# Order of the first loads, an earlier pick and whole last rows in a fused sigmoid attention and mixture-of-depths kernel

## The chip, the cores and the metric

The kernel runs on one core of one Trainium2 chip. The time is the device time of that core in microseconds for one execution, with all loads from and stores to the chip's DRAM in it. The time before is the median of 4 runs, 437.7 us (436.35 to 439.9). A profile shows one more execution.

## The reference

Sigmoid attention is computed for 8 batches of 12 heads, 448 tokens and 64 dims in float32. Its result, put together to 768 columns per token, goes through a mixture of depths: of each batch the 128 tokens with the highest gate score get a two-layer perceptron added, and the other tokens pass through.

```python
# q, k, v: (8, 12, 448, 64); w_gate: (768,); w1: (768, 1024); w2: (1024, 768); capacity: 128
scores = scale * np.matmul(q, k.transpose(0, 1, 3, 2)) - np.log(S)
attn = 1.0 / (1.0 + np.exp(-scores))
x = np.matmul(attn, v)                    # to (B, S, H * D)
scores = np.einsum('bsd,d->bs', x, w_gate)
out = x.copy()
for b in range(B):
    top_idx = np.argpartition(-scores[b], capacity)[:capacity]
    xe = x[b, top_idx]
    h = np.maximum(xe @ w1, 0.0)
    ye = h @ w2
    g = 1.0 / (1.0 + np.exp(-scores[b, top_idx]))
    out[b, top_idx] = x[b, top_idx] + g[:, None] * ye
```

## The kernel before

Everything is written out in one order by hand (`stream`); each engine runs its own instructions in that order and waits on semaphores for what it needs.

Four heads make a quad; there are 24 quads, three to a batch. A stage `s` (0 to 11) works on two quads, 2s and 2s + 1, in seven slots `n`. In a slot `score` computes q times k for 128 rows of keys, half of them from the one quad and half from the other (`chunks` and `column` say which). A slot has four calls of it: `e` is the half of the 64 dims that is summed, `pr` the pair of heads in the quad; the two pairs lie on different rows of the matmul array. `squash` runs ScalarE's sigmoid on one pair's scores. `value` multiplies v with the sigmoids of earlier slots and gathers the result in four banks. So each slot from the fifth on holds score calls, value calls of slots some way back and two sigmoids. `turn` and `turn_first` transpose q and k on VectorE in blocks of 32; `take` transposes the results into `x_b`, from where `store` writes them to `out`.

In stage 0 the slots 0 and 1 use quad 0 alone and the slots 2 and 3 quad 1 alone, so the first slots can do with little data; `outs` is a pair of banks that slots 0 and 2 write, `PA` the pair that slots 1 and 3 write. After slot 3 the banks of `outs` become the banks of the results, and the first value calls are made. `turn_first` takes k in parts: parts 0 and 1 serve the first slots and the middle columns of k, part 2 the ends of k, needed from slot 4.

The perceptron is computed for two batches at a time, by a scheme of seven products in place of eight (`first`, `second`, `first_sums`, `second_sums`), in blocks after slot 3 of the later stages, and after the last stage in `rest`. Before it, `gate_part` and `gate` make a batch's gate scores, `rank` and `place` rank the tokens, `fetch` picks the 128 tokens by an index and `gather` fetches their rows by an indirect DMA on GpSimd's (POOL's) queue. `FETCHED` says after which slot each batch is picked. The results are added into these rows (`xe`), and `scatter` writes them back by another indirect DMA. For the last batch, `scatter_half` writes each half of the 768 columns as soon as its last sum is made.

All other loads go through SyncE's (SP's) queue in the order of the program. A DMA there waits in line for what its tile needs, and for one of eight semaphores: the ninth DMA waits for the first to land, the tenth for the second, and so on. At the start, SP's queue holds: the middle of k of quad 0, q of quad 0, the middle of k of quad 1, q of quad 1 (`load_first`), four blocks of v for the first columns, the ends of both k, four blocks with the rest of v, four gate-weight loads (`constants`), and then k and q of quads 2 and 3 and v of stage 1.

Of the kernel before, what the change touches and what calls it, by code (L numbers as in the profile page):

```python
# [17 lines left out]
def kernel(  # L18
# [89 lines left out]
    def load_first():  # L108

        raw, turned = {}, {}  # L110
        for i in range(2):
            if i:
                both = heads["both"] = moe.tile([P, 6 * KH * P], F32, name="rows_t")
                raw["k", i] = both[:, :TB * Dh]
            else:
                raw["k", i] = head.tile([P, TB * Dh], F32, name="raw_k", bufs=1)
            raw["q", i] = head.tile([P, TB * Dh], F32, name="qT")
            for which, src, at, n in (("k", k, AT, TB - 2 * AT), ("q", q, 0, TB)):
                heads[which, i] = raw[which, i]
                nc.sync.dma_start(  # L120
                    out=raw[which, i][:, at * Dh:(at + n) * Dh],
                    in_=bass.AP(tensor=src.tensor, offset=src.offset + (i * 4 * S + at) * Dh,
                                ap=[[TB * Dh, P], [1, n * Dh]]))
        load_v(0, True)
        for i in range(2):
            nc.sync.dma_start(
                out=raw["k", i].rearrange("p (r d) -> p r d", d=Dh)[:, 0:AT],
                in_=bass.AP(tensor=k.tensor, offset=k.offset + i * 4 * S * Dh,
                            ap=[[TB * Dh, P], [Dh, AT], [1, Dh]]))
            nc.sync.dma_start(  # L130
                out=raw["k", i].rearrange("p (r d) -> p r d", d=Dh)[:, TB - AT:],
                in_=bass.AP(tensor=k.tensor, offset=k.offset + (i * 4 * S + TB - AT) * Dh,
                            ap=[[TB * Dh, P], [Dh, AT], [1, Dh]]))
        load_v(0, False)

    def turn_first(i, *parts):

        t = heads["raw", i].rearrange("p (r e d) -> p e r d", e=2, d=TT)
        kt = heads["k", i]
        for part in parts:  # L140
            if part < 2:
                nc.vector.transpose(kt[:, :, 2 * part:2 * part + 2],
                                    t[:, :, AT + part:AT + part + NA + 2:NA + 1])
                nc.vector.transpose(kt[:, :, 2 * (NA + part):2 * (NA + part) + 2],
                                    t[:, :, NA + part:NA + part + 3:2])
                continue
            for a, r in ((0, 0), (1, TB - AT)):
                nc.vector.transpose(kt[:, :, 4 + a:2 * NA:2], t[:, :, r:r + AT])

    def open_first(i):  # L150
        heads["raw", i] = heads["k", i]
        heads["k", i] = head.tile([P, 2, TB, TT], F32, name="kT")

# [34 lines left out]
    def load_v(s, pairs_too=None):  # L188
# [12 lines left out]
        if s or pairs_too:  # L201
            raw_v[s] = t = t.rearrange("p (h c) -> p h c", h=4)

        def block(x, r, n):
# [126 lines left out]
    def constants():  # L331
        make_identity(nc, iden)
        for a in range(4):
            p = slice(a * TT, (a + 1) * TT)
            nc.sync.dma_start(
                out=wg_b[p],
                in_=bass.AP(tensor=moe_w_gate.tensor, offset=moe_w_gate.offset + a * TT,
                            ap=[[0, TT], [P, HP], [1, TT]]))
        nc.gpsimd.iota(slot_s, pattern=[[0, 1]], base=0, channel_multiplier=1,
                       allow_small_or_imprecise_dtypes=True)  # L340

        for t in (gate_s, *who):
# [11 lines left out]
        nc.gpsimd.tensor_scalar(out=tie, in0=tie, scalar1=slot_s, scalar2=-2.0 ** -126,  # L354
                                op0=ALU.is_lt, op1=ALU.mult)
        nc.gpsimd.tensor_scalar(out=wg_b, in0=wg_b, scalar1=GATE_UP, scalar2=None, op0=ALU.mult)

# [23 lines left out]
    def score(s, n, e, pr, out):  # L381

        for y in range(2):
            x, c, step = chunks(s, n, y)
            r = 2 * column(s, n, y)
            kt = heads["k", 2 * s + x]
            qt = heads["q", 2 * s + x].rearrange(
# [146 lines left out]
    def fetch(b):  # L534

        n = CAP
        idx = moe.tile([P, 1], I32, name="idx", bufs=7)
        got = moe.tile([P, 2], F32, name="got", bufs=5)
# [8 lines left out]
        gather(b)  # L547
        if b == B - 1:
            st[b]["halves"] = [moe.tile([P, 1], I32, name="idx", bufs=7) for _ in range(2)]
            for m in range(2):  # L550
                nc.vector.tensor_scalar(out=st[b]["halves"][m][:n], in0=got[:n, 0:1],
                                        scalar1=2.0, scalar2=float(2 * b * S + m),
                                        op0=ALU.mult, op1=ALU.add)

# [129 lines left out]
    def second_sums(p, key, ps):  # L684
        n = CAP
        left = pairs[p].setdefault("left", [6, 8])
        for x, m in QUARTERS[key]:
            b = 2 * p + x
            cols = slice(m * DH, (m + 1) * DH)
            xe = st[b]["xe"]  # L690
            nc.vector.scalar_tensor_tensor(  # L691
                out=xe[:n, cols], in0=ps[:n, :DH], scalar=st[b]["gate"][:n, 0:1],
                in1=xe[:n, cols], op0=ALU.mult, op1=ALU.add)
            left[x] -= 1
            if b == B - 1:
                parts = st[b].setdefault("parts", [4, 4])
                parts[m] -= 1
                if not parts[m]:
                    scatter_half(b, m)
            elif not left[x]:  # L700
                scatter(b)
# [7 lines left out]


    def scatter_half(b, m):
        n = CAP
        nc.gpsimd.indirect_dma_start(
            out=out[:b + 1].rearrange("b s (m d) -> (b s m) d", m=2),
            out_offset=bass.IndirectOffsetOnAxis(ap=st[b]["halves"][m][:n, 0:1], axis=0),
            in_=st[b]["xe"][:n, m * DH:(m + 1) * DH], in_offset=None)

# [150 lines left out]
    def slot(s, n):  # L868


        if s == 0 and n < NF + 1:
# [3 lines left out]
            psc = PA if n % 2 else outs  # L875
            for e in range(2):
                for pr in (1, 0):
                    score(s, n, e, pr, psc[pr])
            for pr in (1, 0):
                squash(s, n, pr, psc[pr])  # L880
# [105 lines left out]
    def after(s, n):  # L986
# [35 lines left out]
        if s == 0:  # L1022
            if n == 0:
                open_first(1)
                turn_first(1, 0)
# [6 lines left out]
            if n == 4:  # L1032
                turn("k", 2, 3)
                load_v(1)
                load("k", 4)
            if n == 5:
                turn("q", 2, 3)
        if (s, n) in WEIGHTS:
            m, x = WEIGHTS[s, n]
# [19 lines left out]
    RANKED = [(3, 1), None, (6, 1), None, (9, 0), None, (11, 6)]  # L1059
    FETCHED = {(3, 6): 0, (5, 2): 1, (6, 3): 2, (8, 3): 3, (9, 5): 4, (11, 3): 5}  # L1060

    first_outs = ExitStack()

    def stream():
# [4 lines left out]
        nc.vector.memset(bias_s, NEG_LOG_S)  # L1069
        open_first(0)  # L1070
        turn_first(0, 0)
        turn("q", 0)
        turn_first(0, 1)
        pool = first_outs.enter_context(tc.tile_pool(name="ps_o", bufs=1, space=PSUM))
# [47 lines left out]
```

## Time and profile before

| What | Value |
|---|---|
| median of 4 runs | 437.7 us |
| those runs | 436.35, 436.59, 438.82, 439.9 us |
| the profiled execution's own time | 438.38 us |
| its span | 436.6 us |
| granted TensorE clock, mean | 0.994 |
| busy: PE, DVE, ACT, POOL | 424.1, 281.6, 190.9, 49.0 us |
| moved by DMA | 78.64 MB, 180 GB/s in the mean |

PE is TensorE, DVE VectorE, ACT ScalarE, POOL GpSimd and SP SyncE. The span reaches from the first to the last instruction, and the profiled execution's own time is 1.8 us longer. A line of the timeline gives the start, the duration from start to end of the merged instructions, engine, line of the kernel, operation, tiles, shapes and count, and in brackets the engine's idle time before it with what ended it. The chain is the work that ended last, followed back from the end, each piece with its start and length. A line of the table by stretches gives the stretch, its length, the busy time and instruction count of PE, its weight loads, DVE, ACT and POOL, then the granted clock, the busy share of the DMA engines and the GB/s.

### The profile page before, as it was taken

Reading aid. Unit: us, or ns where it says so; the run is one execution under the profiler, and the core shown is the slowest. Engines: PE = TensorE matmul, PEld = TensorE weight load, DVE = VectorE, ACT = ScalarE, POOL = GpSimd, SP = SyncE. Lnnn points to the kernel's source line nnn. Section 1 sums busy time; section 2 is a strip of 40 time slices with the busy share of each in tenths; the row PEclk is TensorE's granted clock in tenths of the full one; section 3 lists DMA queues with packets and bytes.
Section 4 is the critical chain, followed back from the end, with each engine's and each line's share of the span. In section 5 each row is a group of like instructions: output and inputs, shape, how many; then the busy total and the mean of one; then the engine's idle time right before and its main releaser. Section 6 shows DMA issues by size and latency. Waiting matters only on the chain.

```text
span 436.6 us, 14255 instructions
## 1 busy us (share of the span) xinstructions
PE 424.1 (97%) x6324; PEld 253.7 (58%) x6324; DVE 281.6 (64%) x598; ACT 190.9 (44%) x249; POOL 49.0 (11%) x82
## 2 busy tenths in 40 slices
PE   6999999999999999999999999999999999999994
PEld 2565454534666468565447549546445749669852
DVE  3335556792958785976968736755765749982561
ACT  4566666656664642650561661563264330101100
POOL 3000001210110020100202020010020110101002
PEclk9899999999999999999999999999999999999998
DMA  7696837899863998989466896399834990921001
GB/s 211 200 240 203 296 87 142 219 185 248 230 197 80 202 286 254 215 290 225 163 209 196 248 222 140 110 269 268 259 101 98 243 258 24 182 60 74 0 1 72
DMA packets 114985, 78.64 MB, mean 180 GB/s; under 512 B 91436, under 2 KB 100908, under 8 KB 114924
## 3 DMA queue, kind: packets, MB, share of 16 engines
q1 hardware_dynamic: 107948, 62.47, 54.7%
q0 software_dynamic: 3344, 9.54, 7.6%
q10 hardware_dynamic: 3632, 5.74, 5.5%
q8 instruction: 49, 0.80, 0.8%
q14 instruction: 12, 0.10, 0.1%
HBM read 57.25 MB, written 20.48 MB: 178 GB/s over the span
## 4 chain that ended last, share of the span: by engine, by line
PE 93%; DMA 3%; ACT 1%; issue 1%; DVE 0%; SPq 0%; POOLq 0%; ACTq 0%
PE a L391 30%; PE o L423 28%; PE o L616 11%; PE o L680 11%; PE a L616 6%; PE a L680 5%; DMA qT<-in_q_dram 2%; ACT attn L405 1%; PE o L580 1%; PE p L391 1%; DMA out_dram<-xe,idx 1%; DMA out_dram<-attn,idx 1%; PE a L580 0%; SPq L120 0%; POOLq L1117 0%
## 5 line engine op out<-in xcount | busy, mean ns | idle before, releaser
L391 PE MATMUL a<-qT,kT 32*64 32x448 f32 x2624 | 243.1, 539 | 0.4
L405 ACT ACTIVATE attn<-a,bias_s 128x896 f32<-128x896 f32 x162 | 161.7, 1008 | 84.7 <-PE a L391 82.0
L423 PE MATMUL o<-attn,raw_v 32*64 32x448 f32 x1952 | 176.5, 537 | 0.1
L391 PEld LDWEIGHTS a<-qT,kT 32*64 32x64 f32 x2624 | 95.1, 132 | 89.4 <-ACT attn L405 52.9
L423 PEld LDWEIGHTS o<-attn,raw_v 32*64 32x64 f32 x1952 | 69.8, 131 | 28.9 <-issue 23.6
L447 DVE STREAM_TRANSPOSE x_b<-o 128x448 f32<-128x448 f32 x48 | 28.1, 626 | 52.7 <-PE o L423 34.9
L423 PE MATMUL o<-attn,rows_t 32*64 32x448 f32 x448 | 42.2, 538 | 0.8 <-issue 0.8
L632 ACT ACTIVATE hidden<-hidden 128x512 f32<-128x512 f32 x12 | 7.5, 632 | 65.8 <-DVE hidden L629 55.6
L458 DVE TENSOR_REDUCE gate_p<-scr 128x14 f32<-128x448 f32 x48 | 29.8, 621 | 1.7
L629 DVE TENSOR_TENSOR hidden<-o,hidden 128x512 f32<-128x512 f32 x23 | 15.2, 688 | 23.9 <-PE o L616 23.7
L455 DVE TENSOR_TENSOR scr<-x_b,wg_b 128x448 f32<-128x448 f32 x48 | 29.6, 617 | 1.1
L379 DVE STREAM_TRANSPOSE kT<-raw_k 128x448 f32<-128x448 f32 x42 | 24.1, 612 | 7.3 <-PE a L391 7.0
L370 DVE STREAM_TRANSPOSE qT<-qT 128x896 f32<-128x896 f32 x22 | 23.9, 1086 | 6.2 <-DMA qT<-in_q_dram 6.2
L616 PE MATMUL o<-rows_t,spare 128*128 128x128 f32 x216 | 25.6, 276 | 0.0
L616 PEld LDWEIGHTS o<-rows_t,spare 128*128 128x128 f32 x216 | 24.8, 192 | 1.4 <-DVE x_b L447 1.4
L680 PE MATMUL o<-spare,hidden 128*128 128x384 f32 x72 | 24.3, 487 | 0.0
L513 DVE SCALAR_TENSOR_TENSOR scr<-rep,who,tie 128x448 f32<-128x448 f32 (+1 forms) x28 | 19.0, 677 | 7.4 <-DMA rep<-scores 6.6
L691 DVE SCALAR_TENSOR_TENSOR xe<-o,gate,xe 128x384 f32<-128x384 f32 x29 | 16.6, 612 | 9.7 <-PE o L680 9.6
L529 POOL DMA_DIRECT2D ranks<-turned x28 | 14.6, 527 | 70.6 <-DVE turned L526 70.6
L423 PEld LDWEIGHTS o<-attn,rows_t 32*64 32x64 f32 x448 | 16.4, 131 | 7.6 <-issue 7.4
L423 PE MATMUL o<-attn,hidden 32*64 32x448 f32 x224 | 20.2, 535 | 0.0
L616 PE MATMUL o<-rows_t,w_sb 128*128 128x128 f32 x168 | 20.0, 276 | 0.1
(118 smaller groups left out, 392.7 us busy)
## 6 DMA issues: line engine op xcount, KB each, us to landing
qT<-in_q_dram SPq DMA_DIRECT2D x24, 448.0 KB, 5.0
out_dram<-x_b SPq DMA_DIRECT2D x32, 336.0 KB, 8.5
raw_k<-in_k_dram SPq DMA_DIRECT2D x21, 448.0 KB, 5.1
spare<-sum SPq DMA_DIRECT2D x18, 384.0 KB, 6.3
sum<-spare SPq DMA_DIRECT2D x8, 768.0 KB, 7.9
raw_v<-in_v_dram ACTq DMA_DIRECT2D x24, 224.0 KB, 6.6
w_sb<-in_moe_w_dram SPq DMA_DIRECT2D x6, 768.0 KB
rows_t<-in_v_dram SPq DMA_DIRECT2D x8, 224.0 KB, 4.4
```

The costliest lines, as they stand in the source:

```text
L370: nc.vector.transpose(heads["q", i], heads["q", i])
L379: nc.vector.transpose(kt[:, e], t[:, e].rearrange("p (a n) d -> p n a d", a=2))
L391: nc.tensor.matmul(out[y * Dh:(y + 1) * Dh, h % 2, :S], kt[d, e, r:r + 2].rearrange("d r t -> d (r t)"), qt[d, e], start=(e == 0), stop=(e ...
L405: nc.scalar.activation(a, psc[:, :, :S], AF.Sigmoid, bias=bias_s, scale=QK_SCALE)
L423: nc.tensor.matmul(PO[x][pr][j * Dh:(j + 1) * Dh, :S], raw_v[s][rows, 2 * pr + j, at:at + Dh], attn[s, pr, n][rows, j, :], start=((s, x, p ...
L447: nc.vector.transpose(x_tiles[b][:, :, 2 * g + pr, :], PO[x][pr][:, :S].rearrange("p (r t) -> p r t", t=TT))
L455: nc.vector.tensor_tensor(out=tmp, in0=x_tiles[b][:, :, hp, :], in1=wg_b[:, hp:hp + 1, :].to_broadcast([P, TB, TT]), op=ALU.mult)
L458: nc.vector.tensor_reduce(out=gate_parts[b][:, :, hp], in_=tmp, axis=AX.X, op=ALU.add)
L513: nc.vector.scalar_tensor_tensor(out=junk[:n], in0=rep[:n], scalar=own, in1=tie[:n], op0=ALU.subtract, op1=ALU.is_gt, accum_out=place_s[:n ...
L616: nc.tensor.matmul(ps[:, f, :n], w((t * FH + f) * P, P), x[:, t, :n], start=(t == 0), stop=(t == KH - 1))
L680: nc.tensor.matmul(ps[:n, :DH], h[:, t, :n], w(t * DH, DH), start=(t == 0), stop=(t == FH - 1))
L691: nc.vector.scalar_tensor_tensor(out=xe[:n, cols], in0=ps[:n, :DH], scalar=st[b]["gate"][:n, 0:1], in1=xe[:n, cols], op0=ALU.mult, op1=ALU ...
```

## The change

The loads at the start are put in another order. k of quad 1 is loaded whole in one DMA. v is issued after q of quad 0 has been transposed: `load_v` writes one element of v's tile on VectorE, behind these transposes, and the DMA waits for that. The two ends of quad 0's k and the rest of v follow. The gate weights are loaded after slot 4 of stage 0 (`gate_weights`), behind k and q of quads 2 and 3, and v of stage 1 after slot 0 of stage 1, behind q and k of quads 4 and 5.

In slots 0 to 3 of stage 0 the score calls run pair by pair (both halves of the dims of one pair, its sigmoid, then the other pair), where they ran half by half.

Batch 5 is picked after slot 2 of stage 11, where it was slot 3. The last batch's rows are written back by one scatter of whole rows after the last sum, and the two index tiles for the halves go.

```diff
 def load_first():
...
-            for which, src, at, n in (("k", k, AT, TB - 2 * AT), ("q", q, 0, TB)):
+            for which, src, at, n in (("k", k, 0 if i else AT, TB if i else TB - 2 * AT),
+                                      ("q", q, 0, TB)):
...
+    def load_second():
+
         load_v(0, True)
-        for i in range(2):
+        t = heads["k", 0].rearrange("p (r d) -> p r d", d=Dh)
+        for r in (0, TB - AT):
             nc.sync.dma_start(
-                out=raw["k", i].rearrange("p (r d) -> p r d", d=Dh)[:, 0:AT],
-                in_=bass.AP(tensor=k.tensor, offset=k.offset + i * 4 * S * Dh,
-                            ap=[[TB * Dh, P], [Dh, AT], [1, Dh]]))
-            nc.sync.dma_start(
-                out=raw["k", i].rearrange("p (r d) -> p r d", d=Dh)[:, TB - AT:],
-                in_=bass.AP(tensor=k.tensor, offset=k.offset + (i * 4 * S + TB - AT) * Dh,
+                out=t[:, r:r + AT],
+                in_=bass.AP(tensor=k.tensor, offset=k.offset + r * Dh,
                             ap=[[TB * Dh, P], [Dh, AT], [1, Dh]]))
         load_v(0, False)
...
 def load_v(s, pairs_too=None):
...
+        if pairs_too:
+            nc.vector.memset(t[:1, 0, :1], 0.0)
...
 def constants():
         make_identity(nc, iden)
-        for a in range(4):
-            ... (the four loads of wg_b)
...
+    def gate_weights():
+
+        for a in range(4):
+            ... (the four loads of wg_b)
         nc.gpsimd.tensor_scalar(out=wg_b, in0=wg_b, scalar1=GATE_UP, scalar2=None, op0=ALU.mult)
...
 def fetch(b):
-        idx = moe.tile([P, 1], I32, name="idx", bufs=7)
+        idx = moe.tile([P, 1], I32, name="idx", bufs=5)
...
         gather(b)
-        if b == B - 1:
-            st[b]["halves"] = [moe.tile([P, 1], I32, name="idx", bufs=7) for _ in range(2)]
-            for m in range(2):
-                nc.vector.tensor_scalar(out=st[b]["halves"][m][:n], in0=got[:n, 0:1],
-                                        scalar1=2.0, scalar2=float(2 * b * S + m),
-                                        op0=ALU.mult, op1=ALU.add)
...
 def second_sums(p, key, ps):
             left[x] -= 1
-            if b == B - 1:
-                parts = st[b].setdefault("parts", [4, 4])
-                parts[m] -= 1
-                if not parts[m]:
-                    scatter_half(b, m)
-            elif not left[x]:
+            if not left[x]:
                 scatter(b)
...
 def slot(s, n):      # s == 0 and n <= NF
-            for e in range(2):
-                for pr in (1, 0):
+            for pr in (1, 0):
+                for e in range(2):
                     score(s, n, e, pr, psc[pr])
-            for pr in (1, 0):
                 squash(s, n, pr, psc[pr])
...
 def after(s, n):     # s == 0
             if n == 4:
                 turn("k", 2, 3)
-                load_v(1)
+                gate_weights()
                 load("k", 4)
...
+        if (s, n) == (1, 0):
+            load_v(1)
...
-    FETCHED = {(3, 6): 0, (5, 2): 1, (6, 3): 2, (8, 3): 3, (9, 5): 4, (11, 3): 5}
+    FETCHED = {(3, 6): 0, (5, 2): 1, (6, 3): 2, (8, 3): 3, (9, 5): 4, (11, 2): 5}
...
 def stream():
-        open_first(0)
         turn_first(0, 0)
         turn("q", 0)
+        load_second()
         turn_first(0, 1)
```

## The prediction

> **What bounds the kernel now.** I read the page's head and chain first, then the chain piece by piece at both ends, then the timeline of the first 17 us, then the table by stretches for the clock.
>
> ```profile
> span 436.6 us, 14255 instructions
> PE 424.1 (97%) x6324; PEld 253.7 (58%) x6324; DVE 281.6 (64%) x598; ACT 190.9 (44%) x249; POOL 49.0 (11%) x82
> PE 93%; DMA 3%; ACT 1%; issue 1%; DVE 0%; SPq 0%; POOLq 0%; ACTq 0%
> ```
>
> TensorE (PE) is busy 97% of the span and 93% of the chain. Work taken off the other engines in the middle is worth nothing; what can be won lies where the chain leaves PE. There are two such places, the first 16 us and the last 11 us. The start:
>
> ```profile
> 2.12 7.95 DMA qT<-in_q_dram
> 10.09 0.66 DVE qT L375
> 10.88 3.08 PE p L391 x30
> 13.98 1.92 ACT attn L405 x2
> 15.94 1.01 PE o L423 x16
> ```
>
> The second q (I call it q1) is issued at 2.12 and lands at about 10.06. Its first half is transposed, the scores of slot n=2 run, two sigmoids follow, and only then do the first value matmuls start (15.94). From there PE has no large holes.
>
> ```profile
> 10.88 3.12 PE L391 MATMUL p<-qT,kT 32*64 32x448 f32 x32 [2.13 <-DVE qT L375]
> 13.98 1.91 ACT L405 ACTIVATE attn<-p,bias_s 128x896 f32<-128x896 f32 x2 [3.00 <-PE p L391]
> 7.70:11.10 3.40, 1.27 (x32) 0.44 (x24) 1.52 (x4) 3.28 (x4) 0.00 (x0) 1.00 0.86 185
> 11.10:14.50 3.40, 3.40 (x45) 1.67 (x39) 1.86 (x7) 0.52 (x1) 0.00 (x0) 0.51 0.54 137
> ```
>
> PE stood 2.13 us for q1, and ScalarE (ACT) then stood 3.00 us for PE. The two lower lines are stretches: PE was busy 1.27 of 3.40 us, and in the stretch after it the granted clock was 0.51, so slot 2 took 3.1 us where slot 0 took 1.76. The late q1 is paid twice. The end:
>
> ```profile
> 424.98 0.63 DVE xe L691
> 425.61 0.27 issue
> 425.88 3.02 DMA out_dram<-xe,idx
> ...
> 428.93 0.73 issue
> 429.66 2.52 DMA out_dram<-attn,idx
> ...
> 432.23 0.51 issue
> 432.74 1.20 POOLq L1117
> 430.14 0.62 DVE L691 SCALAR_TENSOR_TENSOR attn<-o,gate,attn 128x384 f32<-128x384 f32 x1 [1.44 <-PE o L680]
> 432.96 0.97 POOL L713 DMA_INDIRECT out_dram<-attn,idx  x1 [2.33 <-DMA out_dram<-attn,idx]
> ```
>
> Three scatters stand in a row, each waiting for the landing of the one before. The last rows are ready at 430.76 (430.14 + 0.62), but their second half goes out at 432.96, because the first half had to land.
>
> **The start, step by step.** SP's queue sends k0's middle, q0, k1's middle, q1 and then four blocks of v, 160 KB each, at 2.59 to 4.69. After the change k1 goes whole (448 KB for 256) and v waits for a memset of one element behind q0's transposes. These end at 5.95 (4.78 + 1.17), so v is issued from about 6.1 and, by today's 2.10 us for four issues, until 8.2. Behind the waiting v on SP stand k0's two ends, the rest of v, k2, k3, q2, q3.
>
> *q1.* k0, q0, k1 and q1 are 1,638 kB (decimal) then. By the one-us stretches the queues moved 23, 311, 357, 278 and 302 kB up to 6.0, which is 1,271; the rest at 300 per us is through at 7.2. What lies between bytes moved and landing: q0 (with k0, 721 kB, through at 4.1) landed by 4.78, 0.7 later, with little but plain loads in flight; q1 today (1,442 kB, through at 6.6) landed 3.5 later, with v in flight. So 7.9 by the one, 10.7 by the other. The new q1 resembles q0's case; I take 7.9 to 8.5.
>
> *ACT then sets the pace.* Its first sigmoid starts at 7.28, and four follow each other at 0.90, to 10.99. Slots 2 and 3 can follow without a hole if slot 2's first pair is ready at 10.99. It needs two transposes (0.7 to PE's start) and two score calls: 0.75 + 0.75 + 0.2 for draining, so landing + 2.5; that holds up to 8.5. Slot 2's sigmoids end at 10.99 + 2 x 0.90 = 12.8 instead of 15.9, and the first values start 3.1 earlier. PE's hole falls from 2.13 us to about 0.5, so I expect no halved clock.
>
> The clock has a rule against it: the Trainium skill, "TensorE: Matmul & The Clock Gate", section "HAM oscillation", says that gaps must exceed about 3.4 us to throttle. This trace halved it after 2.13 us. By the rule the drop had another cause and may stay: slot 3 would cost up to 1.4 more, and the sum would be about 1.4 higher. The measured row decides for me.
>
> *Order of the score calls.* The first four slots now do both halves of one pair, then of the other. The pairs use different row groups of PE: slot 0's 32 matmuls start in four groups of eight (5.48, 5.91, 6.28, 6.66), and both pairs are ready at the end, 7.24. If each pair keeps its own rows, pair 1 is ready at 7.2 as now, pair 0 about 0.5 later, behind the other pair's sigmoid of 0.9: nothing. If pair 1 gets the whole array, 0.4 is won. If PE does not look past pair 1, a slot takes 3.0 instead of 1.5 and the front gain is gone. Score and value matmuls of different rows, which alternate in the timeline at 18.02 and 18.10, say that it looks ahead; I take 0.
>
> *v and k0's ends.* v (655 kB) follows q1 at today's mean of 6 to 10 us (289, 187, 216, 238: 232 per us): 7.2 + 2.8 = 10.0, and with 0.7 to the landing 10.7; needed at 12.8. k0's ends (197 kB) 0.9 later: 11.6, and 0.89 + 0.64 for four transposes: 13.1; slot 4 needs them at 13.7. No price. The upper bound goes by today's latencies: 8.2 from issue to landing for v puts it at 15.8; the ends issued at 5.38 served the transpose at about 13.2, 7.8 later, which puts them at 16.6 and the transposes at 18.1, 4.4 too late. The first estimate is nearer, because those 8.2 are spent behind k1 and q1. A rule against it: "DMA: Bandwidth & Descriptors", "Rules for kernel authors", advises issuing a DMA early and waiting late. By it v should stay ahead, and by the upper bound the sum would lose 3.0.
>
> *Gate weights and next v.* Four gate-weight issues (12.76 to 15.47) leave the path of k2; their first reader on VectorE (DVE) was at 42.49: nothing. The next v is moved behind q4, q5 and k5. q4 waits for slot 6's scores (today 26.7, then 23.6), k5 for k4's transpose (24.9), so v is issued at 25.3 to 28. It ends a run of 2,294 kB from 24.6; at 290 per us that is 32.5, with latencies of 8.2 at most 36. Its first reader is at 38.82 today, 35.7 then. Cover 3 us, price 0 to 0.3.
>
> **Middle.** The pick of batch 5 (0.64, 0.69 and 0.15 on DVE) moves from 334.12 into DVE's idle 7.70 us before 331.56. Its gather went out at 336.36, and the six transposes that need it started at 343.53, as the 48 matmuls before them ended: nothing won here, safety gained, and POOL has nothing else to do then. Dropping two tiny DVE index instructions: nothing.
>
> **The end.** One scatter replaces two. It waits for the batch-6 scatter (landed 428.9, earlier than needed) and for the last row update, 430.76; with the 0.29 seen between DVE and POOL it goes out at 431.05, 1.9 before today's 432.96. From there to the span's end were 3.64; a whole row set took 3.02 to land where a half took 2.52, so 4.14: 435.2, a gain of 1.4. Bounds: by the median of such scatters in traffic (3.5) 0.9; with equal landings 1.9.
>
> **Sum.** The profiled execution took 438.38 (span 436.6 and 1.8 around it). 438.38 - 3.1 - 1.4 = 433.9. It is 0.7 above the median of the runs shown, 437.7; carried over to that, 433.2, 1.0% less. About 1% is also what a measurement of this kernel can tell from no change.
>
> **Rivals.** (a) *The start gives back half.* q1 keeps part of its lag and lands at 9.6, so ACT starts slot 2 at 12.1: 1.9 instead of 3.1, or the ends of k0 are a microsecond late. For it: the last parts of a load lag when others are in flight (k1 took until 8.27). Against: v is out of its way. 437.7 - 1.9 - 1.4 = 434.4. (b) *The end gives nothing*: the whole rows take 1.9 longer than a half. Against: 3.02 beside 2.52. 437.7 - 3.1 = 434.6. (c) *v and k0's ends become the wait*, at slots 3 and 4, by the upper bounds: slot 4 starts at 18.1 instead of 16.92, 1.2 later than today; PE stands some 3 us again, and a halved clock over 3.4 us costs 1.7; less 1.4 at the end: 439.2. It decides from v landing after 12.8 and takes the whole gain when the ends' transposes pass 16.9; if the next v is late by the same share it goes on to 442 or more. For it: 640 KB are issued 3.5 us later. Against: the queues are busy either way. (d) *v is not held*: the built order has the wait on DVE at the first v, so this is excluded.
>
> **Numbers.** Forecast 0.55, (a) 0.22, (b) 0.10, (c) 0.13. The forecast lies at the 1% line and its own range is 431.5 to 434; I count 0.48 of it as over 1%, since a shorter last landing or an earlier first sigmoid only add, and 0.07 within. (a) gives 0.05 and 0.17, (b) 0.01 and 0.09, (c) 0.11 slower and 0.02 within. Faster 0.54, same 0.35, slower 0.11. The range, 431.3 to 438.2, holds the forecast, (a), (b) and the milder part of (c).
>
> **What would show it.** Right: the first value matmul at 12.8 to 13.3; no q1 in the chain with more than 6.5 us; clock 1.0 between 11.1 and 14.5; ACT without a hole from 7.28 to about 14.6; one scatter of the last rows issued 0.3 after DVE's last update. Wrong: a PE wait on raw_v or on k0's transposes between 12 and 18 us, a hole before 35.7 at the next v, slots 0 to 3 of 3 us each, or a last landing over 4 us.

## The result, and the profile after

The changed kernel takes 435.42 us (median of 42 runs; 437.93 for the kernel before on the same chip, 68 runs). The ratio is 0.995, with a 95% interval of [0.9934, 0.9966]: 0.5% less, some 2.2 us, where 4.5 were forecast. In two later sets of runs the same kernel gave 0.9895 [0.986, 0.9931] and 0.9935 [0.9906, 0.9963], so the gain is somewhere between 2 and 5 us. The second set's 4.6 us is of the forecast's size; the pieces below show that the forecast's working fails all the same.

Its profiled execution took 433.96 us. The head and the chain of its page:

```profile
span 432.1 us, 14249 instructions
PE 424.3 (98%) x6324; PEld 253.7 (59%) x6324; DVE 281.4 (65%) x597; ACT 190.5 (44%) x249; POOL 48.1 (11%) x81
PE 94%; ACT 2%; DMA 1%; issue 1%; DVE 0%; POOLq 0%; SPq 0%; ACTq 0%
```

PE does the same work; the span is 4.5 shorter. That this is just the number forecast is chance: the pieces below make 2.1 by stage 1, less 0.6, and 1.6 at the end, and the other 1.4 was won between 45 and 320 us, where the two kernels are the same. The start, from the chain of waits:

```profile
1.18 3.47 DMA qT<-in_q_dram
5.38 2.87 PE p L397 x28
8.27 3.70 ACT hidden L411 x4
11.97 1.90 ACT attn L411 x2
13.92 1.01 PE o L429 x16
```

The second q has left the chain, and ScalarE's sigmoids run without a hole from 8.27 to the first values at 13.92 (15.94 before): 2.0 won, not 3.1. PE's clock was first granted in full at 7.6 us (4.3 before), so slot 0's scores took 2.87 where 1.76 was reckoned with. The end, from the timeline:

```profile
427.26 0.62 DVE L691 SCALAR_TENSOR_TENSOR attn<-o,gate,attn 128x384 f32<-128x384 f32 x1 [1.44 <-PE o L680]
428.16 0.96 POOL L700 DMA_INDIRECT out_dram<-attn,idx  x1 [4.19 <-DVE attn L691]
```

One scatter, issued 0.28 after the last row update (427.88); from PE's last product to the span's end it is 5.41 us, before it was 6.98. In between, at slot 4 of stage 1, the new kernel lost 0.6 that the forecast did not have:

```profile
37.11 1.65 PE L429 MATMUL o<-attn,rows_t 32*64 32x448 f32 x12
39.34 1.01 ACT L411 ACTIVATE attn<-a,bias_s 128x896 f32<-128x896 f32 x1 [1.35 <-PE a L397]
40.83 1.01 ACT L405 ACTIVATE attn<-a,bias_s 128x896 f32<-128x896 f32 x1 [0.73 <-PE a L391]
```

The timeline has twelve value matmuls with no scores among them, and ScalarE is idle for 1.35 us before the next sigmoid. The last line is the same sigmoid in the kernel before, with 0.73 idle before it. From stage 1's first sigmoid to this one it is 12.80 us, before 12.19.

### The profile page after: what moved, and what is told of

It reads as the page before. It is cut to its first block, busy times and chain, and to the rows that moved or that the text cites. A ratio compares the mean times of both kernels' runs of the same rounds, so it can differ in the third digit from the quotient of the medians.

```text
span 432.1 us, 14249 instructions
## 1 busy us (share of the span) xinstructions
PE 424.3 (98%) x6324; PEld 253.7 (59%) x6324; DVE 281.4 (65%) x597; ACT 190.5 (44%) x249; POOL 48.1 (11%) x81
## 4 chain that ended last, share of the span: by engine, by line
PE 94%; ACT 2%; DMA 1%; issue 1%; DVE 0%; POOLq 0%; SPq 0%; ACTq 0%
PE a L397 30%; PE o L429 29%; PE o L616 11%; PE o L680 11%; PE a L616 6%; PE a L680 5%; ACT attn L411 1%; PE o L580 1%; ACT hidden L411 1%; DMA qT<-in_q_dram 1%; DMA out_dram<-xe,idx 1%; PE p L397 1%; PE a L580 0%; POOLq L1105 0%; DVE x_b L453 0%
## 5 line engine op out<-in xcount | busy, mean ns | idle before, releaser
L616 PEld LDWEIGHTS o<-rows_t,w_sb 128*128 128x128 f32 x168 | 19.4, 192 | 1.0 <-DVE x_b L453 0.7
```

The lines of the kernel that those rows point to most:

```text
L616: nc.tensor.matmul(ps[:, f, :n], w((t * FH + f) * P, P), x[:, t, :n], start=(t == 0), stop=(t == KH - 1))
```

## The experiments

There are seventeen runs, two to four of them on one chip with the kernel before beside them; four are repeats. A ratio is good to about 0.3%, 1.3 us, so single terms below that were read in the profiles, one for each run. The table holds what I read there, in us. "Slot 4" is the start of that slot's first sigmoid in stage 0; "6 to 1.0" goes from slot 6's first sigmoid to stage 1's first, "1.0 to 1.4" from there to the first sigmoid of stage 1's slot 4 (the "five slots" of the expectations; 12.19 where nothing is lost), "tail" from the start of PE's last product to the end of the span.

| kernel | q1 transposed | first sigmoid | slot 4 | 6 to 1.0 | 1.0 to 1.4 | tail |
|---|---|---|---|---|---|---|
| before | 10.09 | 7.28 | 19.08 | 3.37 | 12.19 | 6.98 |
| after | 9.38 | 8.27 | 17.06 | 3.37 | 12.80 | 5.41 |
| e1_tail | 8.10 | 6.99 | 15.78 | 4.60 | 12.19 | 5.42 |
| e2_front | 10.03 | 7.61 | 17.71 | 3.37 | 13.53 | 6.99 |
| e3_halves_first | 8.76 | 7.10 | 16.44 | 3.37 | 14.07 | 5.41 |
| e4_no_hold | 10.98 | 7.73 | 20.08 | 3.37 | 13.21 | 5.42 |
| e5_after_again | 10.88 | 7.02 | 19.94 | 3.37 | 13.76 | 5.40 |
| e6_v1_early | 9.73 | 7.56 | 17.41 | 3.37 | 12.19 | 5.41 |
| e7_v1_early_halves | 9.04 | 7.96 | 16.72 | 3.37 | 12.19 | 5.41 |
| e8_tail_again | 9.30 | 7.09 | 16.98 | 5.62 | 12.90 | 5.41 |
| e9_best_again | 8.70 | 7.55 | 16.38 | 3.37 | 12.19 | 5.41 |
| e10_gates_early | 10.36 | 7.92 | 18.04 | 3.37 | 12.19 | 5.41 |
| e11_k1_split | 6.93 | 7.34 | 16.03 | 3.36 | 12.19 | 5.42 |
| e12_old_first_loads | 8.86 | 7.91 | 16.61 | 3.37 | 12.18 | 5.41 |
| e13_v1_one_later | 7.12 | 7.06 | 15.75 | 3.37 | 13.08 | 5.41 |
| e14_tail_gates_late | 9.51 | 7.32 | 17.19 | 3.37 | 12.19 | 5.42 |
| e15_after_third | 8.38 | 7.26 | 16.05 | 3.37 | 13.18 | 5.40 |
| e16_v1_behind_k4 | 11.32 | 7.52 | 20.42 | 3.37 | 12.19 | 5.41 |
| e17_v1_behind_k4_spent | 7.68 | 7.63 | 16.33 | 3.37 | 13.70 | 5.41 |

### The change in two halves: e1_tail, e2_front

e1_tail is the kernel before with one scatter of the last rows:

```
-            if b == B - 1:
-                ... (parts, scatter_half)
-            elif not left[x]:
+            if not left[x]:
                 scatter(b)
```

> The kernel before with one change: the last rows go back by one scatter. First theory (the end gains what the sum said, and it is the start that gains less over many executions than in the two profiled ones): 1.4 to 1.6 us less than before, ratio 0.9965, the scatter issued 0.9 after batch 7's last update and the span ending some 4.1 after that. Second theory (the end is what was overrated, and the start gains its 2 to 3 in nearly every execution): 0 to 0.5 less, ratio 0.999 to 1.000.

e2_front is the changed kernel with the halves and the old pick again, so that only the loads and the order of the scores are new:

```
+            if b == B - 1:
+                ... (parts, scatter_half)
-    FETCHED = {..., (11, 2): 5}
+    FETCHED = {..., (11, 3): 5}
```

> The changed kernel with the two half scatters and the later pick put back, so that the order of loads and of score calls alone is left. First theory: about 1.0 us less than before (ratio 0.9975), because the kernel before does not always lose what its profiled execution lost at its start. Second theory: 2 to 2.5 less (ratio 0.995).

Measured: e1_tail 0.9982 [0.9958, 1.0006], e2_front 1.0005 [0.9975, 1.0035]. The tail is 5.42 against 6.99, so the scatter is worth 1.57, and the column shows the same in every profile. The loads won nothing that the times show. e1_tail's profile says why; its start is the old code, and its sigmoids read:

```profile
6.99 1.90 ACT L405 ACTIVATE hidden<-p,bias_s 128x896 f32<-128x896 f32 x2 [4.21 <-PE p L391]
8.79 1.91 ACT L405 ACTIVATE hidden<-a,bias_s 128x896 f32<-128x896 f32 x2
10.68 1.90 ACT L405 ACTIVATE attn<-p,bias_s 128x896 f32<-128x896 f32 x2
12.47 1.91 ACT L405 ACTIVATE attn<-a,bias_s 128x896 f32<-128x896 f32 x2
15.78 1.01 ACT L405 ACTIVATE attn<-a,bias_s 128x896 f32<-128x896 f32 x1 [1.40 <-PE a L391]
```

No hole in the first eight sigmoids, no halved clock, slot 4 at 15.78: the start that I forecast for the change, made by the start code of the kernel before. The profiled execution of the kernel before, at 19.08, had been a bad draw.

### Parts of the start undone: e3_halves_first, e4_no_hold

Both are the changed kernel; e3_halves_first has the score calls half by half again, e4_no_hold lacks the memset that holds v back.

```
-            for pr in (1, 0):
-                for e in range(2):
+            for e in range(2):
+                for pr in (1, 0):
                     score(s, n, e, pr, psc[pr])
```

> The changed kernel with the score calls of slots 0 to 3 half by half again, as before. If the order of the calls is neutral, as the sum had it: the same as the changed kernel, ratio 0.995 to before. If pair by pair costs time where PE is at half clock (slot 0 took 3.09 in the profiled execution and ACT started at 8.27, not at 7.28): 0.5 to 1 faster than the changed kernel, ratio 0.993.

```
-        if pairs_too:
-            nc.vector.memset(t[:1, 0, :1], 0.0)
```

> The changed kernel without the memset, so that v is issued at 2.6 us, behind q1 and not behind q0's transposes; k1 still whole, the rest as changed. If v in flight is what makes q1 late: q1 lands at about 10.5 again, the first values start at 15 to 16 and the ratio is 0.998, near what the end alone gives. If q1's lag has another origin (packets that take about 1 us each already before v flows): q1 within 0.5 of 9.4, first values as in the changed kernel, ratio 0.995.

Measured: 0.9946 [0.9917, 0.9975] and 0.9964 [0.9934, 0.9995], beside 0.995 for the changed kernel. The order of the calls is worth nothing that shows. e4_no_hold had a late q1 (10.98) and a halved clock; one profile could not say whether that was the missing hold or a draw. All four profiles so far with the late next v had 12.8 to 14.1 in the column "1.0 to 1.4".

### The next v at its old place: e5_after_again, e6_v1_early, e7_v1_early_halves, e8_tail_again

e5_after_again and e8_tail_again repeat the changed kernel and e1_tail. The other two:

```
             if n == 4:
                 turn("k", 2, 3)
+                load_v(1)
                 gate_weights()
                 load("k", 4)
...
-        if (s, n) == (1, 0):
-            load_v(1)
```

e7_v1_early_halves also has the score calls half by half, as in e3_halves_first.

> The changed kernel again, nothing edited, on the same chip as the three runs beside it. Theory: the start of one execution is a draw. The forecast's 3.1 us at the start came from a profiled execution of the kernel before that had drawn badly (second q transposed at 10.09, slot 4's first sigmoid at 19.08, halved clock); other executions with the same start code reach slot 4 at 15.8. Then the changed kernel stays at its 2 us gain, ratio 0.993 to 0.997, of which 1.6 is the tail (5.4 us from PE's last product to the span's end), and in this new profile slot 4's first sigmoid falls somewhere between 16 and 18.5, not at 17.06 again. Rival: the start gain is real and the middle takes it back: slot 4 again at 17.0 to 17.2, a ratio like before, and the loss at the next v again at 12.8 us for five slots.

> The changed kernel with the next v issued at its old place (stage 0, slot 4, ahead of the next k), all else changed. Theory: the late next v costs 0.6 to 1.9 us, because its four blocks land at 33 to 36 us and five slots of stage 1 take 12.8 to 14.1 us in the profiles so far where the kernel before took 12.2. Then those five slots take 12.0 to 12.4 here, PE doesn't wait for it, and the time is 0.6 to 1.9 us below that of the changed kernel run beside it, about 434. Rival: the slow slots belong to something else that arrives late there (q4, q5 or k5, which now queue behind v again): five slots still take over 12.7, and the time is that of the changed kernel within 0.5.

> As the run with the next v at its old place, and the score calls of the first slots half by half again instead of pair by pair. Theory: the order of the calls is worth 0 to 0.5 us and the next v 0.6 to 1.9, and they add: 433.5 to 434.5, the fastest of these. Rival: the order of the calls matters not at all, as the forecast had it, and this agrees with its neighbour within 0.4.

> The kernel before with one whole scatter of the last rows in place of two halves, again, as a second look at its start, which is the old one. Theory: the start is a draw, the old code included; slot 4's first sigmoid lies anywhere from 15.8 to 19.1, its first full clock anywhere from 4 to 8 us, and the time is 1.0 to 1.6 below the kernel before by the tail alone (5.4 us from PE's last product to the end, for 7.0). Rival: the first look (slot 4 at 15.78) was the lucky one and the late q the rule: slot 4 at 18.5 or later with a halved clock behind it, and what the changed kernel has on this run, 1 to 2 us, is its start.

Measured: 0.9895 [0.986, 0.9931], 0.9917 [0.9883, 0.9951], 0.9893 [0.9859, 0.9928] and 0.994 [0.991, 0.9971]. The times don't separate them, though the profiles do: 12.19 in both with v early, 13.76 in the changed kernel beside them. The expected 434 for e6_v1_early was met (434.2), the order by time was not, since e5_after_again came out faster (432.6). As for the start, the same code that had slot 4 at 17.06 had it at 19.94 in e5_after_again, with q1 at 10.88 and a halved clock, while the old code was at 16.98 in e8_tail_again. There a second price appeared, in the column "6 to 1.0". DVE's timeline of e8_tail_again, and then of the changed kernel:

```profile
21.73 1.11 DVE L370 STREAM_TRANSPOSE qT<-qT 128x896 f32<-128x896 f32 x1
25.62 1.11 DVE L370 STREAM_TRANSPOSE qT<-qT 128x896 f32<-128x896 f32 x1 [2.78 <-DMA qT<-in_q_dram]
```

```profile
20.28 2.06 DVE L376 STREAM_TRANSPOSE qT<-qT 128x896 f32<-128x896 f32 x2
```

In the one, q3 lands 2.8 us after DVE is free, and the scores of stage 1's first slot (the expectations call it slot 7) wait for it: 5.62 instead of 3.37. In the other, both are there. In e8_tail_again q2 and q3 were issued at 15.94, behind four gate-weight issues that held SP from 13.05 to 14.93; in the changed kernel at 13.56. (Whether the issues' time or their packets delayed q3 the more is not told apart.) In the profiles with the old place, this wait is hidden where the start is late (19.08 at slot 4) and paid where it is early (15.78 and 16.98).

### Which part of the start matters: e9 to e12

The base is e7_v1_early_halves, run again as e9_best_again. e10_gates_early puts the four gate-weight loads back into constants(), ahead of k2. e11_k1_split splits the second k again:

```
-            for which, src, at, n in (("k", k, 0 if i else AT, TB if i else TB - 2 * AT),
+            for which, src, at, n in (("k", k, AT, TB - 2 * AT),
...
 def load_second():
+        for i in range(2):
+            ... (both ends of k0, then of k1)
```

e12_old_first_loads does that too, without the memset, and calls load_second() right behind load_first(), so that SP issues the first loads in the order of the kernel before.

> The version with the next v at its old place and the score calls half by half, unchanged, as the base for the three runs beside it. The five slots of stage 1 up to slot 4 take 12.19 us again, q3's transpose follows q2's at once, and the tail is 5.41; ratio to the kernel before 0.986 to 0.993. If it comes out above 0.995 the first look was a good draw.

> The base with the four gate-weight loads back ahead of the loads for stage 1 on SP's queue, as in the kernel before. Theory: what the start gains is not the first q but these four issues, 1.9 to 3.0 us on SP, which leave the path of k2, k3, q2 and q3. In the two profiles that had the old place and an early start, q3's transpose came at 23.4 and 25.6 and slot 7's scores waited for it (from slot 6's first sigmoid to stage 1's first, 4.60 and 5.62 us instead of 3.37). So here the same wait appears, q3 is transposed 2 us or more after q2 instead of right behind it, 4.0 to 5.5 instead of 3.37, and the run is 0.7 to 2 us slower than the base. Rival, the forecast's own step: the gate weights cost nothing there, 3.37 again and the base's time within 0.5.

> The base with the second k split again: its middle ahead of the second q, its two ends behind the held v. 98 KB each of 128 x 192 then leave the path of the second q. Theory: the hold's gain for the second q is eaten by loading the second k whole; with the split it is transposed at 8.0 to 9.0 instead of 8.8 to 10.9 (mean of six profiles 9.6), the ends still land before slot 4 needs them, and the run is 0.3 to 0.8 us faster than the base. Rival: the second q's lag comes from single slow packets on some DMA queues, whatever the bytes ahead: 8.8 to 10.9 again, and the base's time within 0.5.

> The base with the first loads as in the kernel before: second k split, v issued right behind the second q with nothing held, all else as in the base. Theory: over nine profiles the second q is transposed at 8.1, 9.3 and 10.1 with these loads and at 8.8 to 10.9 with the held ones, so the hold wins nothing: 8 to 10.5 here and the base's time within 0.7. Rival, the forecast: v in flight delays the second q by 2 us, its transpose is at 10 or later, slot 2's first sigmoid at 13 or later, and the run is 2 to 3 us slower than the base.

Measured: 0.993 [0.9907, 0.9954], 0.9917 [0.989, 0.9944], 0.9925 [0.9903, 0.9947] and 0.9911 [0.9884, 0.9939]. e12_old_first_loads speaks against the hold: with the old first loads q1 came at 8.86 and slot 4 at 16.61, and nothing was lost. It is one draw; averages follow below. e11_k1_split brought q1 to 6.93, the earliest of all, and won no time that shows. At the start it could win little, since the sigmoids, which start at 7.34, set the pace; and its profile lost 1.1 us against the kernel before's behind slot (1, 4), where only the pick was changed. e10_gates_early failed as a test: it drew a late start (slot 4 at 18.04), under which the gate weights hide, as in the kernel before.

### The price of the late v, and the gate weights alone: e13, e14, e15

e13_v1_one_later is the changed kernel with load_v(1) behind slot (1, 1) in place of (1, 0). e14_tail_gates_late is e1_tail with the gate weights issued behind the next v:

```
-        for a in range(4):
-            ... (the four loads of wg_b, in constants())
...
                 load_v(1)
+                gate_weights()
                 load("k", 4)
```

e15_after_third is the changed kernel again.

> The changed kernel with the next v issued one slot of stage 1 later still, 3.0 us after its place there. Theory: in the changed kernel this load is already the last to arrive, so every further microsecond is paid: the five slots up to stage 1's slot 4 take 15 to 17 us (12.19 where v is on time, 12.80 and 13.76 in the changed kernel), TensorE waits there for raw_v's blocks, and the run is 2 to 3 us slower than the changed kernel beside it, at or just below the kernel before. Rival, the forecast: the cover is 3 us, so the slot takes at most 12.8 to 13.8 again and the time moves by less than 1 us.

> The kernel before with the whole scatter and with the four gate-weight loads moved behind the next v, and nothing else. Theory: with these loads out of the way k2, k3, q2 and q3 are issued 2 to 3 us earlier, q3's transpose follows q2's at once, and from slot 6's first sigmoid to stage 1's first it is 3.37 us (4.60 and 5.62 with the whole scatter alone); the next v at its old place gives 12.19 for the five slots after it. Then this small part of the change with the tail makes all that the whole change makes, 0.988 to 0.994 of the kernel before. Rival: without the held first loads the start stays where it was and only the tail's 1.6 shows: 4 us or more at slot 7 again, or 0.996 and above.

> The changed kernel again, as the base for the two beside it. By the theory five slots of stage 1 take 12.6 to 14.1 us, slot 4's first sigmoid lies 8.7 to 8.9 us behind the first sigmoid of the kernel if the second q is transposed by 9.4 and later if not, and the ratio lies at 0.990 to 0.996. Rival: a ratio near 0.985 to 0.989, as the forecast had it.

Measured: 0.9946 [0.9912, 0.998], 0.9957 [0.9925, 0.9988] and 0.9935 [0.9906, 0.9963]. e13_v1_one_later was a miss: SP runs ahead of PE, and with nothing between the two places it issued v at 25.52, no later than in e15_after_third (26.08); it lost 0.89 there, like its neighbour (0.99). e14_tail_gates_late did as the theory said in the profile, 3.37 and 12.19. Its ratio lies between the two expectations and within two of the changed kernel's three intervals: the whole scatter and four later loads make what the whole change makes, as far as the times can tell. e15_after_third drew the start that was forecast: sigmoids at 7.26, 10.96, 12.75, first values at 12.91.

### What PE waits for at slot (1, 4): e16_v1_behind_k4, e17_v1_behind_k4_spent

e13_v1_one_later held a hint. All of v's packets had ended by 33.30, and the first value matmul on rows_t ran at 35.41: v was there, and 0.89 was lost all the same. Wherever PE stood, it did so behind the same instruction, the 1217th of PE's records in the trace (matmuls, weight loads and its sequencer's own), with no semaphore behind it ("issue" in the timeline). The page says what comes at such intervals: 49 packets of queue q8, "instruction", 0.80 MB in all, 16 KB each, for 12,648 matmuls and weight loads: one packet of PE's code for every 256 or so. e16_v1_behind_k4 issues the next v early, behind k4. e17_v1_behind_k4_spent adds, at the changed kernel's place, loads that nobody reads:

```
             if n == 4:
                 turn("k", 2, 3)
                 gate_weights()
                 load("k", 4)
+                load_v(1)
...
-        if (s, n) == (1, 0):
-            load_v(1)
+        if (s, n) == (1, 0):      # e17_v1_behind_k4_spent only
+            ... (the same four blocks of v into w2_sb)
```

> The changed kernel with the next v issued straight behind k4, some 5 us earlier than in the changed kernel, ahead of q4, q5 and k5. In eight profiles with the next v late, its last packet ended 0.5 to 1.6 us ahead of a 16 KB packet of TensorE's instruction code, that packet came 5.1 to 6.1 us after TensorE had passed the instruction at which the others' came after 2.2 to 3.4, and v itself was there 1.5 us before its first reader. Theory: not v's landing but the code packet behind v's bytes stops TensorE at slot (1,4). Then with v early the fourth code packet comes under 4 us after its crossing, and five slots of stage 1 take 12.19 us. Rival: something else in this stretch; the five slots take 12.6 or more again.

> The same, and at the place where the changed kernel issues its next v, four loads of the same bytes and form into a part of the second weights' room that is not yet in use (it is loaded again later): data that nobody reads. Theory: TensorE's code packet queues behind them as it did behind the next v: it comes 5 us or more after its crossing, TensorE stands at the same instruction, and five slots of stage 1 take 12.6 to 14 us, although the real v landed long before. Rival: the next v's own landing sets the loss in the changed kernel, by whatever semaphore; then nothing waits for the spent loads, and the five slots take 12.19.

(The profiles with the next v late are seven, not eight.) Measured: 12.19 and 13.70; times 0.9916 [0.9884, 0.9947] and 0.9933 [0.9897, 0.997]. PE's timeline, first of e16_v1_behind_k4, then of e17_v1_behind_k4_spent:

```profile
40.06 0.72 PE L429 MATMUL o<-attn,rows_t 32*64 32x448 f32 x4
40.36 0.55 PE L397 MATMUL a<-qT,kT 32*64 32x448 f32 x4
40.46 0.69 PE L429 MATMUL o<-attn,rows_t 32*64 32x448 f32 x4
40.74 0.55 PE L397 MATMUL a<-qT,kT 32*64 32x448 f32 x4
```

```profile
36.38 1.46 PE L429 MATMUL o<-attn,rows_t 32*64 32x448 f32 x11
38.39 0.53 PE L429 MATMUL o<-attn,rows_t 32*64 32x448 f32 x1 [0.55 <-issue]
38.40 1.28 PE L397 MATMUL a<-qT,kT 32*64 32x448 f32 x16
```

Values and scores alternate in the first; in the second PE runs out behind eleven values and starts again at 38.39, 1.5 us after the code packet (35.82, 1.11 long) was there. The DMA queues of e17_v1_behind_k4_spent from 28.0 to 35.7, and then to 37.0 (packets, MB, share of the 16 engines):

```profile
q1 hardware_dynamic: 1029, 2.11, 106.2%
```

```profile
q1 hardware_dynamic: 193, 0.36, 95.2%
q8 instruction: 1, 0.02, 5.3%
```

PE passed its 961st instruction at 29.98. In the next 5.7 us the engines were full of data and no code packet got through; it came at 35.82, as the spent loads ran out (504 of their 512 packets had ended by 35.21, the last at 36.27). The real v had landed by 26.71, nine microseconds before its first reader, and nobody waits for the spent loads. So loads in flight ahead of the code are the cause, and not who reads them. In nineteen profiles the delay from the 961st instruction to the next code packet orders the loss:

| delay, us | kernels | lost at slot (1, 4), us |
|---|---|---|
| 0.79 to 3.72 | eleven, all without a late load there | 0 |
| 5.07, 5.11 | after, e13_v1_one_later | 0.61, 0.89 |
| 5.39, 5.39 | e4_no_hold, e15_after_third | 1.02, 0.99 |
| 5.59 | e2_front | 1.34 |
| 5.84, 5.84 | e5_after_again, e17_v1_behind_k4_spent | 1.57, 1.51 |
| 6.07 | e3_halves_first | 1.88 |

Up to 3.72 us it is free, from 5.07 on it is paid. (PE needs 6.7 us for the 256 instructions; the packet takes 1, and 1.4 to 1.7 pass before PE starts. By estimate, 6.7 less 2.5, some 4.2 us should be free.) The Trainium skill, "Runtime: NRT & Kernel Launch", section "Instruction fetch mechanics", says that engines fetch code in 16 KiB blocks of 256 instructions by a DMA queue of their own, and that crossing a block is mostly hidden. The blocks agree with the trace. "Mostly hidden" held at this block in eleven of nineteen profiles, and not in the eight with a late load.

No version tried is shown to be faster than the changed kernel. e7_v1_early_halves and its repeat e9_best_again lose neither at stage 1's first slot nor at (1, 4); their profiled spans, 429.8 and 430.0 us, are with that of e6_v1_early (429.4) the three shortest, but their ratios are 0.9893 and 0.993 where the changed kernel has 0.9895 to 0.995.

## Why the prediction was wrong, step by step

**The start, 3.1 us: the step that failed is the sum, "438.38 - 3.1 - 1.4", carried over to the median.** The subtrahend was one execution's misfortune. The median was close to that execution's total, and I took this for a sign that its start was typical too; but its total holds many draws, and the start was a bad one. The reckoning within the start was right where q1 came in time: "10.99", "12.8" and a gain of 3.1 were met to 0.1 us by e15_after_third. They were met or bettered by e1_tail with the old loads (10.68, 12.47). From q1's landing to the first sigmoid of slot 2 it was 2.58 in e2_front, e6_v1_early and e7_v1_early_halves, where 2.5 was reckoned (the terms written there add up to 2.4). Over the five profiles with the old first loads slot 4 comes at 17.13 on average (15.78 to 19.08), over the twelve with v held and k1 whole at 17.35 (15.75 to 20.42).

**q1 at 7.9 to 8.5: failed.** Over the same profiles q1 is transposed at 9.17 and 9.28 on average; with the hold it came at 7.12 to 11.32. The choice between two lags (0.7 with only plain loads in flight, 3.5 with v) put the blame on v, and against v speak e12_old_first_loads and these averages. Why q1's last packets lag as they do in some executions stays open. That k1 loaded whole takes back what the hold gives is supported by e11_k1_split (6.93) alone, one draw.

**The clock: the measured row held, not the rule.** In the first 18 us the clock fell in four of nineteen profiles, behind waits for q1 of 2.13, 2.26, 2.66 and 2.80 us, and stayed behind waits of up to 1.78. What I forecast, no halved clock, holds where q1 is early.

**Order of the score calls, 0; v and k0's ends, no price: right.** In no profile does PE wait for raw_v or for k0's ends between 8 and 18 us.

**Gate weights, "nothing": failed, and to the good side.** I looked at the first reader of the weights and at the queue's length, not at who stood behind them on SP. The 1.9 to 3.0 us of issues that leave the path of q2 and q3 are worth 0 under a late start, and 1.2 (e1_tail) and 2.2 (e8_tail_again) under an early one. e8_tail_again and e14_tail_gates_late differ in the place of these loads alone; slot 4 came at 16.98 and 17.19, and the column "6 to 1.0" reads 5.62 and 3.37. Without this step an earlier start would have been lost here again.

**Next v, "Cover 3 us, price 0 to 0.3": failed.** The cover was real, if thinner: v's last packet ended at 35.34, its first reader ran at 36.72. The price, 0.6 to 1.9 (1.2 on average over the seven profiles), came from another passenger of the same queues, PE's own code, which no row of the page named as a wait.

**The middle, "nothing won": not contradicted.** Between 322 and 354 us, around the earlier pick, PE's lead over the kernel before stays between 2.9 and 3.0 us. No run has the pick alone.

**The end, 1.4 (0.9 to 1.9): right.** 1.57 in every profile; issued 0.28 after the last update (0.29 reckoned).

**The sum, as it should have been:** 1.6 at the end, nothing for the first loads, some 1.4 from the gate weights (0, 1.2 and, with 0.7 more that e8_tail_again lost one block of code earlier, 3.0 in the three profiles that have the old place and the old loads), less 1.2 for the next v: 1.8, beside 2.2 measured with the first set and 2.8 to 4.6 with the others. (The block before the 961st instruction takes PE 6.05 us in e14_tail_gates_late, and in e8_tail_again its code packet came 4.24 us after the crossing. Reckoned as above, 3.55 are free and 0.69 is paid: an estimate, not tested.) The sum doesn't reach 4.6, and why the sets differ stays open. Single profiles differ by more than any term here behind slot (1, 4), where only the pick was changed up to the tail: up to the last sigmoid e6_v1_early gained 3.8 us there on the kernel before, and e11_k1_split lost 1.1. Rivals (a) and (b), at 434.4 and 434.6, came nearest in time, but not by their reasons. (a) had q1's landing nearly right (9.6, on average 9.28) and took its gain from the same bad draw; the end, which (b) put at nothing, gave what the sum had.

## What to carry to other kernels

A hole in one profiled execution is a price only if other executions have it too; before a gain is read off, ask how the waits behind it were drawn, and carry over the steps that every execution shares (the tail) apart from those that vary (a load's last packets). When an issue is moved on a queue, reckon the price of what stands behind it as well as that of its own reader. Loads that keep all DMA engines busy can hold up PE's own code, even when every load is in time for its reader. By these runs, a stretch is at risk when it is longer than PE takes for a block of its code, less some 2.5 us (an estimate: 4.2 us here). A wait by "issue" on PE beside such a stretch is the sign.

## What the runs showed of the hardware

**Code packets queue behind data.** As above: 5.1 to 6.1 us from crossing to packet, 0.6 to 1.9 us lost. The same sign stands a second time in this kernel, nine blocks later (behind the 3521st instruction, around 95 us). Gaps of over 0.65 us between PE's starts come there only with packets 4.3 us or more after the crossing; the longest are 1.84 (e2_front, 5.48) and 1.29 (the kernel before, 4.96). That is part of what varies from run to run.

**In these profiles the clock changes at the ends of windows of 3.4 us whose place differs from execution to execution.** The first full clock came at 4.3 to 7.6 us, and changes followed in steps of 3.4 from there: in e4_no_hold PE's hole ended at 11.77, and the clock fell at 13.3. With the windows so laid, in the first 18 us it was halved after those in which PE had been busy 0.74, 0.99, 1.27 and 1.53 us, and stayed after 1.86, 2.10, 2.28 and more. Two neighbours, e5_after_again and e8_tail_again, from the table by stretches (us, PE busy, PEld, DVE, ACT, POOL busy, clock, DMA share, GB/s):

```profile
8.40:11.80 3.40, 0.74 (x16) 0.16 (x8) 1.42 (x4) 2.32 (x3) 0.00 (x0) 1.00 0.73 167
11.80:15.20 3.40, 3.40 (x40) 1.86 (x46) 1.80 (x7) 0.36 (x1) 0.00 (x0) 0.51 0.79 212
```

```profile
7.70:11.10 3.40, 1.86 (x48) 0.74 (x40) 1.56 (x4) 3.10 (x4) 0.00 (x0) 1.00 1.08 213
11.10:14.50 3.40, 2.92 (x65) 1.08 (x48) 1.29 (x4) 2.62 (x3) 0.00 (x0) 1.00 0.53 114
```

In these first windows the busy time and the length of the gap order the profiles alike. The end of the kernel sets them apart, here in e7_v1_early_halves:

```profile
423.40:426.82 3.42, 1.48 (x5) 0.57 (x3) 0.70 (x2) 0.00 (x0) 0.96 (x1) 1.00 0.00 0
426.82:430.23 3.41, 0.00 (x0) 0.00 (x0) 0.00 (x0) 0.00 (x0) 0.00 (x0) 1.00 0.28 115
```

PE was busy for only 1.48 us and kept its clock in the next window; it had been idle since 424.88, 1.94 us up to the window's end. In e10_gates_early PE was idle from 428.18 to its window's end at 430.24, 2.06 us, and the clock fell. So the busy time alone doesn't decide, and the idle stretch orders all of these cases, with the step between 1.94 and 2.06 us. The products at the end have another shape than those at the start, so that it is the gap that decides is not shown. The Trainium skill, "TensorE: Matmul & The Clock Gate", Part 1, speaks of a free-running activity window, which fits; its section "HAM oscillation" asks for gaps of over 3.4 us, where 2.06 up to the window's end was enough here.
